# A one-core FNet-plus-MLP kernel: a second staging place, four turning places, an earlier split and an earlier build step

## The chip, the cores and the metric

The kernel runs on one core of a Trainium2 chip. The metric is the device time of one execution, in microseconds (us); a kernel's time is the median of several executions.

The engines are named as the profile names them: PE is TensorE (matmuls), PEld its weight loads, DVE VectorE, ACT ScalarE, POOL GpSimd, SP SyncE, which issues most DMAs. In the trace each engine runs its instructions in program order, and they wait for one another through semaphores. A DMA queue belongs to the engine that issues it; POOL's is `q0 software_dynamic`, SP's `q1 hardware_dynamic`.

## The reference

```python
x  = A_x                                   # 1 x 2048 x 640, fp32
xn = layernorm(x)                          # no scale, no shift
a, b = xn @ hid_re.T, xn @ hid_im.T        # 640 x 640 each
fnet = seq_re @ a - seq_im @ b             # 2048 x 2048 each
mlp  = gelu(xn @ w1 + b1) @ w2 + b2        # 640 -> 1536 -> 640
return x + fnet + mlp
```

All data are fp32 and one output of 2048 x 640 is returned.

## The kernel before

**Products.** Each fp32 operand is split into a high part, rounded to the matmul's fp32r format, and a low part, the rest. `split` (L154) does it with two instructions: ACT writes the high part (L160), DVE subtracts it from the source (L161). `product` (L274) then needs three matmuls, high x high (L277), high x low (L278) and low x high (L279), which add into one PSUM bank of 128 x 512. There are eight banks.

**Order of the work.** The schedule is written out by hand: an engine executes instructions in the order in which the Python code issues them, and there is no scheduler. The code interleaves the preparation of later stages with the matmuls of the present one. So a late instruction delays all that stands behind it on its engine, even where that has nothing to do with it.

1. *MLP, token blocks 0 and 1* (512 tokens each): hidden units by `hidden`, GELU, second matrix by `output`. The five outputs of a block lie in banks 3 to 7 (`oacc`).
2. *MLP, hidden layer of blocks 2 and 3*, six pairs of units q = 0 to 5, with a scheme that saves matmuls: `head(q)`, `mid(q)` and `finish(q)`. `PB[q]` says which banks a pair uses; the banks go from pair to pair, so a pair's first matmul into a bank waits until what lay there is read. In `mid`, DVE adds a shared term to two banks (L428, called from L850 and L851); the second of these reads bank z2, into which the first product of `finish` ("t4" with "a22", L855) then goes. `act` (L834) applies GELU and parks the results. Beside it `prep_w` (L396) turns and splits the hidden-dimension matrices and stores them through POOL's DMA queue (`wit`, L394), from five slots of one tile in rotation; it fills a slot again once its store has landed.
3. *MLP, second layer of blocks 2 and 3*: steps n = 0 to 23, 12 units each. Its moving operand is one of three places `HP`, filled by `split_h(p)` (L1053) for pair p of units. Block 2 gathers in banks 0 to 4, block 3 in banks 5, 6, 7, 3 and 4. At n = 12 block 3 starts with its first two units: first into banks 5, 6 and 7 (18 matmuls), then into banks 3 and 4 (12 matmuls), which have to be free of block 2's outputs by then.
4. *Sequence stage*: blocks of the sequence matrices, whose raw rows SP loads (`load_a`, L452) and DVE turns (`turn`, L484) into places `r01` and `rt2`, whose forms `form` (L511) splits.

**Beside stage 3: the builds.** `beside_second(n)` (L1130) issues, among the matmuls, eight builds of the normalised input's forms for stage 4. `load_xr(k)` (L543) loads two tiles of 128 x 640 from `xs` on SP's queue, the first four builds are `formed(k)` at n = 2, 4, 6 and 8: `build` (L561) computes an "ab" form of 128 x 2560 and a "c" form of 128 x 1792, and POOL's queue stores them to `forms_ab` and `forms_c` (L1122, L1123). The c form is put in the place that `homes_c` (L623) names; in the kernel before it is `xcst`, under the tag `tw1`, for each of the four, and the next build's first write there (ACT, L582) waits until the store of the one before has landed. What stands behind a build in program order, on ACT and on DVE: after the fourth (n = 8) come `split_h(6)` (n = 9, needed by PE at n = 12), parts a and b of build 4 (n = 9, from tiles loaded by `load_xr(4)`, issued at n = 6), `split_h(7)` (n = 11), and then the five outputs of block 2 (`outs(2, (3, 4, 0, 1, 2))`, n = 11).

**Outputs of a block.** `outs` (L861) calls `add_block` (L341) for each of five output banks: ACT adds the bias in place (L344), DVE turns the bank into a place `yt` (L347), POOL adds that to `xo` (L349). For block 1 the first output (bank 3) goes by itself (L1064), and the other four in `rest` (L1066) inside `mid(0)`, through the two halves of the tile `AB` in turn. `zs` is a tile of 128 x 3840, seven and a half places of 512 columns, with the sources of stage 2's operands.

**Turn to stage 4** (L1188 to L1273). When PE has done stage 3, ACT copies the five outputs of block 3 with their bias into `ob` (L1247); then follow build 7's part b (L1269: one subtraction and two splits), the turning of piece 2 into `rt2` (whose bytes hold weights that PE reads until the end of stage 3), and build 7's part c. ACT gets to what stands behind L1247 only when PE has finished block 3.

Of the kernel before, what the change touches and what calls it, by code (L numbers as in the profile page):

```python
# [11 lines left out]
F32R = mybir.dt.float32r  # L12
# [3 lines left out]
P = 128  # L16
# [10 lines left out]
def kernel(  # L27
# [43 lines left out]
    TB = 512  # L71
# [24 lines left out]
    NK = 4  # L96
# [57 lines left out]
    def split(hi, lo, src, perm=False):  # L154

        h, l, s = (hi, lo, src)
        if perm:
            h, l = chunked(hi), chunked(lo)
            s = src.rearrange("p (q c i) -> p q c i", q=Q, i=B)
        nc.scalar.activation(h, s, AF.Copy)  # L160
        nc.vector.tensor_tensor(l, s, h.bitcast(F32), op=ALU.subtract)  # L161
# [61 lines left out]
    AB = mr.tile([P, 2, TB], F32, name="ab")  # L223
# [117 lines left out]
    def add_block(dst, e, acc, name, eng=nc.gpsimd, bias=None, yt=None):  # L341

        if bias is not None:
            nc.scalar.activation(acc, acc, AF.Identity, bias=bias)  # L344
        if yt is None:
            yt = rows.tile([P, TB], F32, tag="yt", bufs=2, name=name)
        nc.vector.transpose(yt, acc)  # L347
        d = dst[:, :, e * B : (e + 1) * B]
        eng.tensor_tensor(d, d, yt.rearrange("p (n i) -> p n i", i=B), op=ALU.add)  # L349


    A = {}
# [74 lines left out]
    def add(dst, a, b, op=ALU.add):  # L427
        nc.vector.tensor_tensor(dst, a, b, op=op)  # L428
# [111 lines left out]
    builds = [(h, c) for h in (1, 0) for c in range(NK)]  # L540
# [20 lines left out]
    def build(k, what="abc"):  # L561
        h, c = builds[k]
        b0, b1_ = [r.rearrange("p (q c i) -> p c q i", q=Q, i=B) for r in xr[k]]
        if "a" in what:
            A["xab", c] = homes_ab[k]()
        if "c" in what:
            A["xc", c] = homes_c[k]()
        ab, xc = A["xab", c], A.get(("xc", c))
        if k == len(builds) - 1 and what == "b":
            A["sums"] = out_pool.tile([P, 2, 9 * P], F32, tag="zo", bufs=1, name="sums")  # L570
        tmp = A["sums"][:, (0, 1, 0, 1, 0, 0, 1, 1)[k]]

        def seen(ap):
            return ap.rearrange("p (c q i) -> p c q i", q=Q, i=B)

        n1, m2, t3, t4, b5 = (
            seen(tmp[:, lo * P : (lo + w) * P]) for lo, w in ((0, 2), (2, 2), (4, 2), (6, 2), (8, 1))
        )

        def part(dst, lo, w, src, negative=False):  # L580
            h_, l_ = (seen(dst[:, i, lo * P : (lo + w) * P]) for i in range(2))
            nc.scalar.activation(h_, src, AF.Copy, scale=-1.0 if negative else 1.0)  # L582
            if negative:
                nc.vector.scalar_tensor_tensor(
                    l_, src, -1.0, h_.bitcast(F32), op0=ALU.mult, op1=ALU.subtract
                )
            else:
                add(l_, src, h_.bitcast(F32), ALU.subtract)

        b11, b12, b21, b22 = b0[:, 0:4:2], b0[:, 1:5:2], b1_[:, 0:4:2], b1_[:, 1:5:2]  # L590
        if "b" in what:
            add(n1, b11, b12, ALU.subtract)
        if "a" in what:
            part(ab, 0, 3, b0[:, 0:5:2])
        if "c" in what:
            add(m2, b22, n1)
        if "a" in what:
            part(ab, 3, 3, b1_[:, 0:5:2])
        if "c" in what:
            add(t3, b22, b12, ALU.subtract)  # L600
        if "b" in what:
            part(ab, 8, 2, b22)
        if "c" in what:
            add(t4, m2, b21, ALU.subtract)
        if "b" in what:
            part(ab, 6, 2, n1)
        if "c" in what:
            add(b5, b1_[:, 4:5], b0[:, 4:5], ALU.subtract)
            part(xc, 0, 2, m2, True)
            part(xc, 2, 5, seen(tmp[:, 4 * P :]))  # L610


    def staged(lo):
        return lambda: A["asb"][:, lo : lo + 20 * P].rearrange("p (a b) -> p a b", a=2)

    def at_xab(c):
        return lambda: place(f"xab{c}", (P, 2, 10 * P))
# [2 lines left out]
        return lambda: A["kept", c]  # L620

    homes_ab = [staged(0), at_xab(0), at_xab(2), staged(0), at_xab(0), at_xab(1), at_xab(2), at_xab(3)]
    homes_c = [lambda: A["tw"].tile([P, 2, 7 * P], F32R, tag="tw1", bufs=1, name="xcst")] * NK  # L623
    homes_c += [lambda c=c: A["xcp", c // 2 * 2][:, c % 2] for c in range(NK)]

    zeros = rows.tile([P, TB], F32, tag="yt", bufs=2, name="zeros")
# [107 lines left out]
    def load_rq(q):  # L734
        if q >= NF // 2:
            return
        RQ[q] = A["xf"].tile([P, 4, 2 * P], F32, tag="rq", bufs=1, name=f"rq{q}")
        v = w1.rearrange("(q c i) f -> q i c f", q=Q, i=B)
        for k in range(Q):
            nc.sync.dma_start(RQ[q][k * B : (k + 1) * B], v[k, :, :4, 2 * q * P : 2 * (q + 1) * P])  # L740

    def sums_w1(q):
        if q >= NF // 2:
            return
        r = RQ[q]
        low = r[:, 0:2].rearrange("p c (g f) -> p g c f", g=2)
        high = r[:, :, P:].rearrange("p (k c) f -> p k c f", k=2)
        add(low, high, low, ALU.subtract)
        add(r[:, 2:4, P:], r[:, 2:4, P:], r[:, 0:2, :P], ALU.subtract)
        add(r[:, 2:4, :P], r[:, 2:4, :P], r[:, 2:4, P:], ALU.subtract)  # L750

    def split_w1(q):
        if q >= NF // 2:
            return
        TW[q] = A["tw"].tile([P, 2, 8 * P], F32R, tag=f"tw{q % 2}", bufs=1, name=f"tw{q}")
        split(TW[q][:, 0], TW[q][:, 1], RQ.pop(q).rearrange("p a b -> p (a b)"))
        TW[q] = TW[q].rearrange("p a (c f) -> p a c f", c=4)
# [22 lines left out]
    def pair(k, q, w, x_, first):  # L780
        n = 1 if x_ in ("oa", "ob") else 2
        for cc in range(n):
            f = FX[x_, cc]
            product(bank(k), weights(q, w, cc), (f[:, 0], f[:, 1]), first and cc == 0, cc == n - 1, not first)
# [49 lines left out]
    def act(q, blk, k):  # L834
        y, d, x2, z2, w_ = PB[q]
        src = ((x2, y), (z2, w_))[blk][k]
        u = 2 * q + k
        nc.scalar.activation(park(q, blk, k), bank(src), AF.Gelu_apprx_tanh, bias=b1c[:, u : u + 1])
# [14 lines left out]
    def finish(q):  # L853
        y, d, x2, z2, w_ = PB[q]
        pair(z2, q, "t4", "a22", False)  # L855
        pair(z2, q, "o1", "ob", False)
        pair(y, q, "b22", "s4", False)
        pair(y, q, "o2", "oa", False)
        pair(w_, q, "o2", "ob", False)

    def outs(t, order, yt=None, done=True):  # L861
        for n, e in enumerate(order):
            add_block(
                xo[t], e, oacc[t][e], f"ot{t}_{e}", bias=b2c[:, e : e + 1], yt=yt(n) if yt else None
            )
        for k, (c0, c1) in enumerate(YCOLS if done else ()):
            nc.sync.dma_start(ys[k][t], xo[t][:, :, c0:c1])
# [185 lines left out]
    def split_h(p):  # L1053

        blk, u = (0, 2 * p) if p < NF // 2 else (1, LATE[2 * (p - NF // 2)])
        h = HP[p % 3]
        split(h[:, :, 0], h[:, :, 1], both[blk, u])
        for k in range(2):
            HU[blk, u + k] = h[:, k]
# [4 lines left out]
    outs(1, (0,), yt=lambda n: AB[:, 0], done=False)  # L1064

    def rest():  # L1066
        outs(1, (2, 1, 3, 4), yt=lambda n: AB[:, (n + 1) % 2])

    mid(0, rest)
    forms_s4()  # L1070
    head(1)
# [4 lines left out]
    for q in range(1, NF // 2):  # L1076
        p = q - 1
        if not p % 2:
            act(p, 0, 0)
        sums_w1(q + 1)  # L1080
        act(p, 0, 1)

        def between():
            split_w1(q + 1)
            load_rq(q + 2)
            act(p, 1, 0)
            act(p, 1, 1)

        mid(q, between)
        if q < NF // 2 - 1:  # L1090
            head(q + 1)
        else:
            second(2, 0, 0, HU[0, 0])
            split_h(1)
            for u in (2, 3):
                split_w2(u)
                raw_w2(u + 4, u - 2)
        for k in late_steps.get(q, ()):
            prep_w(k)
        finish(q)  # L1100
        if q == 4:
            split_h(0)
            prep_w(14)
            for u in range(2, 6):
                raw_w2(u, u - 2)
# [96 lines left out]
    def fr_tile(shape, tag, name, dtype=F32):  # L1202
        return fr.tile(list(shape), dtype, tag=tag, bufs=1, name=name)
# [38 lines left out]
            nc.sync.dma_start(A[which, c][:, :, cols].bitcast(F32), src[c][:, :, cols])  # L1242


    ot = [fr_tile((P, 2, TB), tag, f"ob{k}") for k, tag in enumerate(("u1_0", "u2_0", "v1_0"))]
    for e in (3, 4, 0, 1, 2):
        nc.scalar.activation(ot[e // 2][:, e % 2], oacc[NT - 1][e], AF.Identity, bias=b2c[:, e : e + 1])  # L1247
# [18 lines left out]
    def late_block(e):  # L1266
        add_turned(xo[NT - 1][:, :, e * B : (e + 1) * B], turned(ot[e // 2][:, e % 2], f"ot{NT - 1}_{e}"))

    build(len(builds) - 1, "b")  # L1269
    A["rt2"] = place("rt2", (P, 2, 2, 2, TB), F32)  # L1270
    turn(2, 0)
    turn(2, 1)
# [370 lines left out]
    for kind, what in stages:  # L1643
        b = blocks.index(what) if kind == "s" else b
# [63 lines left out]
```

## Time and profile before

| | us |
|---|---|
| median of 3 executions | 864.68 (864.55 to 865.17) |
| the profiled execution's own time | 865.7 |
| its span, first to last instruction | 863.9 |
| PE busy | 845.8 |
| DVE busy | 659.7 |
| ACT busy | 354.3 |
| POOL busy | 45.1 |

The profile's times count from the start of the span. A timeline row gives start, duration, engine, line, operation, written tile <- read tiles, shapes, count of instructions that were merged into the row, and in brackets the idle time of the engine before it with what ended it. The end of a matmul is modelled, and matmuls overlap: in an unbroken run they start 0.23 us apart though each is shown 0.39 us long.

### The profile page before, as it was taken

The numbers are of one execution on the slowest core, as the hardware profiler recorded it, in microseconds if no ns is written. First come the engines' busy times: TensorE is split into PE (matmuls) and PEld (weight loads), VectorE is DVE, ScalarE is ACT, GpSimd is POOL, SyncE is SP. The second block draws the span as 40 slices with busy tenths as digits, with TensorE's granted clock in tenths as the row PEclk, the third lists the DMA queues.
The fourth block names the chain that finished last, engine by engine and source line by source line (L and its number), as shares of the span: only waits on it lengthen the run. The fifth ranks groups of instructions, "written<-read, shape, count | busy, mean of one in ns | idle before, by whom it ended". The sixth has DMA issues, their size and how long they took to land.

```text
span 863.9 us, 10322 instructions
## 1 busy us (share of the span) xinstructions
PE 845.8 (98%) x3711; PEld 696.9 (81%) x3711; DVE 659.7 (76%) x831; ACT 354.3 (41%) x495; POOL 45.1 (5%) x65
## 2 busy tenths in 40 slices
PE   8999999999999799999999999999999999999997
PEld 6888888878878588788888888888888888888885
DVE  7555756766658585988988787998977898885686
ACT  7353634455665444344434333332322423223241
POOL 0000312021211030000000000000000000000000
PEclk9999999999999899999999999999999999999999
DMA  6757798747669976939663659854665869804464
GB/s 183 218 146 185 167 228 233 189 90 191 199 225 371 329 155 138 191 97 231 150 168 86 175 145 307 212 108 125 170 184 175 256 176 233 310 19 177 122 180 95
DMA packets 209219, 158.45 MB, mean 183 GB/s; under 512 B 82896, under 2 KB 182736, under 8 KB 208656
## 3 DMA queue, kind: packets, MB, share of 16 engines
q1 hardware_dynamic: 199936, 136.16, 61.5%
q0 software_dynamic: 3952, 20.71, 6.0%
q10 hardware_dynamic: 5280, 0.92, 0.5%
q8 instruction: 29, 0.48, 0.2%
q14 instruction: 22, 0.18, 0.1%
HBM read 114.76 MB, written 42.99 MB: 183 GB/s over the span
## 4 chain that ended last, share of the span: by engine, by line
PE 87%; issue 6%; DVE 2%; DMA 2%; POOL 1%; ACT 1%; SPq 0%; POOLq 0%; ACTq 0%; DVEq 0%
PE banks L278 26%; PE banks L279 26%; PE banks L277 26%; PE banks L301 9%; DMA forms_c<-xcst 1%; POOL wit L394 1%; DMA x<-in_A_x_dram 0%; DVE rt L488 0%; DMA raw<-in_A_dft_seq_re_dram 0%; POOL xo L349 0%; PE banks L664 0%; DVE hs L161 0%; DVE st L185 0%; DVE wz L428 0%; POOL forms_ab L1122 0%
## 5 line engine op out<-in xcount | busy, mean ns | idle before, releaser
L278 PE MATMUL banks<-as,xab 128*128 128x512 f32 x411 | 160.0, 389 | 0.8 <-DVE as L161 0.8
L277 PE MATMUL banks<-as,xab 128*128 128x512 f32 x411 | 159.9, 389 | 0.0
L279 PE MATMUL banks<-as,xab 128*128 128x512 f32 x411 | 159.9, 389 | 0.0
L160 ACT ACTIVATE as<-r 128x1024 fp32r<-128x1024 f32 x80 | 85.1, 1064 | 175.9 <-PE banks L279 148.3
L161 DVE TENSOR_TENSOR as<-r,as 128x1024 fp32r<-128x1024 f32 x80 | 97.2, 1216 | 38.7 <-ACT as L160 38.7
L278 PEld LDWEIGHTS banks<-as,xab 128*128 128x128 f32 x411 | 77.1, 188 | 17.2 <-DVE as L161 1.3
L277 PEld LDWEIGHTS banks<-as,xab 128*128 128x128 f32 x411 | 77.1, 188 | 16.2
L279 PEld LDWEIGHTS banks<-as,xab 128*128 128x128 f32 x411 | 77.1, 188 | 16.0
L277 PE MATMUL banks<-as,xc 128*128 128x512 f32 x224 | 87.1, 389 | 0.0
L278 PE MATMUL banks<-as,xc 128*128 128x512 f32 x224 | 87.1, 389 | 0.0
L279 PE MATMUL banks<-as,xc 128*128 128x512 f32 x224 | 87.1, 389 | 0.0
L160 ACT ACTIVATE as<-rt 128x1024 fp32r<-128x1024 f32 x32 | 34.1, 1064 | 69.8 <-PE banks L279 57.8
L301 PE MATMUL banks<-xtt,xab 128*128 128x512 f32 x240 | 56.7, 390 | 0.0
L301 PEld LDWEIGHTS banks<-xtt,xab 128*128 128x128 f32 x240 | 44.9, 188 | 9.5 <-DVE xtt L161 0.2
L277 PEld LDWEIGHTS banks<-as,xc 128*128 128x128 f32 x224 | 42.0, 188 | 8.8
L278 PEld LDWEIGHTS banks<-as,xc 128*128 128x128 f32 x224 | 42.0, 188 | 8.7
L279 PEld LDWEIGHTS banks<-as,xc 128*128 128x128 f32 x224 | 42.0, 188 | 8.7
L161 DVE TENSOR_TENSOR as<-rt,as 128x1024 fp32r<-128x1024 f32 x32 | 38.8, 1213 | 5.3 <-ACT as L160 5.3
L488 DVE STREAM_TRANSPOSE r<-raw 128x1024 f32<-128x1024 f32 x32 | 39.5, 1240 | 3.4 <-PE banks L279 2.8
L160 ACT ACTIVATE as<-u 128x1024 fp32r<-128x1024 f32 (+1 forms) x24 | 22.1, 921 | 48.1 <-PE banks L279 48.1
L320 DVE TENSOR_TENSOR hs<-ab,hs 128x512 fp32r<-128x512 f32 x24 | 17.6, 732 | 31.6 <-ACT hs L318 29.4
L161 DVE TENSOR_TENSOR as<-u,as 128x1024 fp32r<-128x1024 f32 (+1 forms) x24 | 24.9, 1043 | 18.8 <-ACT as L160 18.8
(333 smaller groups left out, 1631.6 us busy)
## 6 DMA issues: line engine op xcount, KB each, us to landing
raw<-in_A_dft_seq_re_dram SPq DMA_DIRECT2D x64, 256.0 KB, 5.2
raw<-in_A_dft_seq_im_dram SPq DMA_DIRECT2D x64, 256.0 KB, 5.1
ws<-wit SPq DMA_DIRECT2D x15, 384.0 KB, 4.7
x<-in_A_x_dram SPq DMA_DIRECT2D x16, 320.0 KB, 4.1
xs<-x SPq DMA_DIRECT2D x64, 80.0 KB, 1.8
xo<-in_A_x_dram SPq DMA_DIRECT2D x16, 320.0 KB, 6.1
xab<-wit SPq DMA_DIRECT2D x13, 384.0 KB, 4.4
wit<-wstp POOLq DMA_DIRECT2D x12, 384.0 KB, 4.2
```

The costliest lines, as they stand in the source:

```text
L160: nc.scalar.activation(h, s, AF.Copy)
L161: nc.vector.tensor_tensor(l, s, h.bitcast(F32), op=ALU.subtract)
L277: nc.tensor.matmul(acc, wh, mh, start=first, stop=False, skip_group_check=goes_on)
L278: nc.tensor.matmul(acc, wh, ml, start=False, stop=False, skip_group_check=goes_on)
L279: nc.tensor.matmul(acc, wl, mh, start=False, stop=last, skip_group_check=goes_on)
L301: nc.tensor.matmul(acc, W1[i][:, a, j * P : (j + 1) * P], XT[j][:, b], start=n == 0, stop=n == len(steps) - 1)
L320: nc.vector.tensor_tensor(hs[:, 1], a, hs[:, 0].bitcast(F32), op=ALU.subtract)
L394: nc.gpsimd.dma_start(wits[w][j], t[:, :, :n].bitcast(F32))
L488: nc.vector.transpose(held(pieces[g][2], u).rearrange("p c (n i) -> p c n i", i=B), r.rearrange("p n (c i) -> p c n i", i=B))
```

## The change

There are four edits. None changes what is computed, and the number of matmuls, splits, stores and loads stays the same.

1. The c form of the fourth build goes to the place with tag `tw0`; the first three stay in `tw1`. `tw0` held stage 2's weights of even pairs, and after them the parked units 8 to 11 of block 2, which `split_h(4)` and `split_h(5)` read (n = 5 and n = 7).
2. The four outputs of block 1 in `rest` are turned into places 4, 5, 0 and 1 of `zs` in place of the two halves of `AB`.
3. `split_h(0)` is issued after `finish(3)`, ahead of pair 4's work, in place of after `finish(4)`, where it stood in front of `prep_w(14)`.
4. Build 7's part b is issued ahead of the five ACT copies into `ob`, in place of behind them.

```diff
-    homes_c = [lambda: A["tw"].tile([P, 2, 7 * P], F32R, tag="tw1", bufs=1, name="xcst")] * NK
+    homes_c = [
+        lambda c=c: A["tw"].tile([P, 2, 7 * P], F32R, tag="tw0" if c == 3 else "tw1", bufs=1, name=f"xcst{c}")
+        for c in range(NK)
+    ]
...
     def rest():
-        outs(1, (2, 1, 3, 4), yt=lambda n: AB[:, (n + 1) % 2])
+        free = (4, 5, 0, 1)
+        outs(1, (2, 1, 3, 4), yt=lambda n: A["zs"][:, free[n] * TB : (free[n] + 1) * TB])
...
         finish(q)
+        if q == 3:
+            split_h(0)
         if q == 4:
-            split_h(0)
             prep_w(14)
...
+    build(len(builds) - 1, "b")
     ot = [fr_tile((P, 2, TB), tag, f"ob{k}") for k, tag in enumerate(("u1_0", "u2_0", "v1_0"))]
     for e in (3, 4, 0, 1, 2):
         nc.scalar.activation(ot[e // 2][:, e % 2], oacc[NT - 1][e], AF.Identity, bias=b2c[:, e : e + 1])
...
-    build(len(builds) - 1, "b")
     A["rt2"] = place("rt2", (P, 2, 2, 2, TB), F32)
     turn(2, 0)
     turn(2, 1)
     build(len(builds) - 1, "c")
```

In the built kernels PE's, POOL's and SP's instructions stand in the same order before and after; on ACT and DVE the only instructions that change place are those of edits 3 and 4.

## The prediction

> **What bounds the kernel now.** I read the page first, then PE's waits, then the timelines of each engine around each wait.
>
> ```profile
> span 863.9 us, 10322 instructions
> PE 845.8 (98%) x3711; PEld 696.9 (81%) x3711; DVE 659.7 (76%) x831; ACT 354.3 (41%) x495; POOL 45.1 (5%) x65
> ...
> PE banks L277 <- ACT hs L160: 5.7, 1, 5.7
> ...
> PE banks L278 <- DVE as L161: 0.8, 1, 0.8
> PE banks L277 <- DVE banks L428: 0.8, 1, 0.8
> PE banks L277 <- ACT banks L794: 0.6, 1, 0.6
> ```
>
> PE is busy all but 18.1 us, and the change leaves its matmuls as they are. So an edit is worth the waits of PE that it takes away, less those that it makes. Beyond the start-up there are few: one of 5.7 us, and some below 1 us. A second, third and fourth view place them.
>
> ```profile
> 292.38 0.39 PE L279 MATMUL banks<-xtt,rt 128*128 128x512 f32 x1
> 298.49 0.80 PE L277 MATMUL banks<-hs,xc01w 128*128 128x512 f32 x1 [5.72 <-ACT hs L160]
> 299.75 0.79 PE L278 MATMUL banks<-hs,xc01w 128*128 128x512 f32 x1 [0.46 <-DVE hs L161]
> 300.34 0.63 PE L279 MATMUL banks<-hs,xc01w 128*128 128x512 f32 x1
> ...
> 305.40 0.39 PE L277 MATMUL banks<-hs,xc01w 128*128 128x512 f32 x1
> ...
> 284.38 11.96 DMA forms_c<-xcst
> ...
> 288.30 0.29 DVE L428 TENSOR_TENSOR asb<-xr,xr 128x128 f32<-128x128 f32 x1
> 298.47 1.23 DVE L161 TENSOR_TENSOR hs<-pb,hs 128x1024 fp32r<-128x1024 f32 x1
> ...
> 296.44 1.04 ACT L582 ACTIVATE xcst<-asb 128x256 fp32r<-128x256 f32 x2 [10.22 <-DMA forms_c<-xcst]
> 297.39 1.04 ACT L160 ACTIVATE hs<-pb 128x1024 fp32r<-128x1024 f32 x1
> ...
> 360.00:860.00 500.00, 497.68 (x2195) 411.53 (x2194) 420.00 (x386) 172.50 (x175) 0.00 (x0) 1.00 0.64 171
> ```
>
> The last row is a window's busy times (and instructions) of PE, PEld, DVE, ACT and POOL, then PE's granted clock. It gives the unbroken pace: 2195 matmuls in 500 us, 0.228 us each. PE ends block 2 with the matmul at 292.38 and could start block 3 at 292.61, but starts at 298.49, and its 19th matmul there, the first into bank 3, comes at 305.40 where the pace would give 292.61 + 18 x 0.228 = 296.7. **This pause costs 8.7 us**: 5.9 before the first matmul and 2.8 after it, for the wait on DVE and for matmuls that start 0.43 us apart (300.34 to 303.32 holds seven such steps). Its cause stands in the other rows. ACT, in the fourth build, waits 10.22 us until the third build's c form has left the one staging place, a store of 11.96 us. `split_h(6)` stands behind it on ACT and DVE, and PE needs that.
>
> **The change part by part.**
>
> *Edit 1, second staging place.* In the order of the built instructions, ACT's and DVE's waits on that store are gone and none is added; the readers of `tw0` stand earlier on the same engines. DVE has the fourth build's sums ready at 288.6 (row 288.30). ACT then needs 1.04 at most for the c form's two parts (row 296.44) and 1.04 for `hs`: 290.7. DVE follows, 1.23 for its half: 291.9. PE's first two matmuls need them at 292.6 and 292.8, so this wait ends, with 0.9 us to spare. What is late next stands behind it on both engines: build 4's first parts, `split_h(7)`, and block 2's outputs, whose banks 3 and 4 PE needs with its 19th matmul.
>
> ```profile
> L558 SPq DMA_DIRECT2D xr<-xs x2: 345/360/376, 282.2 to 282.6; - x2
> ...
> DMA to landing us min/median/max: 8.5/10.0/11.6
> ...
> 298.34 1.23 ACT L582 ACTIVATE xab<-xr 128x384 fp32r<-128x384 f32 x3
> 300.39 1.05 ACT L160 ACTIVATE xtt<-pb 128x1024 fp32r<-128x1024 f32 x1
> ...
> 301.55 1.22 DVE L161 TENSOR_TENSOR xtt<-pb,xtt 128x1024 fp32r<-128x1024 f32 x1
> 302.69 1.31 DVE L347 STREAM_TRANSPOSE ot<-banks 128x512 f32<-128x512 f32 x2
> ```
>
> Build 4's two tiles are issued at 282.2 and 282.6 and take 8.5 and 11.6 us: the second lands at **294.2**. In the kernel before that was no matter, ACT began these parts at 298.34. Now it is there at about 291 and waits for the second tile. From 294.2: two of the three parts in row 298.34, 0.85; a fourth, smaller part, some 0.3 by their size; `split_h(7)` on ACT, 1.05, then on DVE, 1.22, with ACT's first bias beside it; then the first turning of row 302.69, 0.7. That makes 298.3 for bank 3. Bank 4 follows 0.6 later, and PE wants it three matmuls, 0.7, later. So PE runs on from 292.6, and pauses 1.6 us ahead of its 19th matmul, at 298.3 in place of 305.40: **7.1 us earlier, not 8.7**. By the kernel's own rows this end does not move with PE, only with the landing.
>
> Does that pause slow the matmuls after it? Row 300.34 shows half pace after 5.72 us of idling; waits of under 1 us (rows below) cost one longer matmul, 0.50 for 0.39. Bounds: 0.1 and 2.8 us, or 856.3 and 859.0 at the end. I take 0.1, since 1.6 is nearer to 0.8 than to 5.7. The Trainium skill, "TensorE: Matmul & The Clock Gate", Part 1 on the clock gate, has a threshold for this: the clock halves after an idle window of about 3.4 us. By it the sum stays at 0.1; the rows above agree on both sides of it, and none shows a pause between 0.8 and 5.7.
>
> *Edit 2, four turning places.*
>
> ```profile
> 182.21 1.36 DVE L347 STREAM_TRANSPOSE ab<-banks 128x512 f32<-128x512 f32 x2 [1.28 <-ACT banks L344]
> ...
> 185.58 0.72 DVE L347 STREAM_TRANSPOSE ab<-banks 128x512 f32<-128x512 f32 x1 [0.52 <-POOL xo L349]
> 186.22 1.26 DVE L428 TENSOR_TENSOR banks<-banks,fifth 128x512 f32<-128x512 f32 x2
> 176.13 1.29 DVE L161 TENSOR_TENSOR xtt<-zs,xtt 128x512 fp32r<-128x512 f32 x2 [0.43 <-ACT xtt L160]
> ...
> 187.39 1.79 DVE L161 TENSOR_TENSOR xtt<-zs,xtt 128x512 fp32r<-128x512 f32 x2
> ...
> 185.11 0.50 PE L277 MATMUL banks<-r,tw 128*128 128x512 f32 x1 [0.39 <-DVE ab L347]
> 187.54 0.50 PE L277 MATMUL banks<-r,tw 128*128 128x512 f32 x1 [0.77 <-DVE banks L428]
> ...
> 200.59 0.85 DVE L372 STREAM_TRANSPOSE wz<-wz 128x640 f32<-128x640 f32 x1 [1.75 <-DMA wz<-in_A_dft_hid_im_dram]
> ...
> 209.79 1.29 DVE L428 TENSOR_TENSOR banks<-banks,fifth 128x512 f32<-128x512 f32 x2
> ...
> 212.16 0.39 PE L277 MATMUL banks<-r,tw 128*128 128x512 f32 x1
> ```
>
> A wait costs its idle time, 0.16 of overlap (0.39 less 0.23) and 0.11 in the longer first matmul: 0.66 and 1.04 here, 1.7 together. Without the wait for POOL, DVE turns the four banks 0.64 apart from 182.21 (two in 1.36, starts 0.64 apart) and begins the additions at 184.8 in place of 186.22, ending them at 186.05. PE reaches the second of these points at 185.9, so 0.3 stays and 1.4 goes. Twenty-five us later there is a new bound: the same additions of pair 2 end at 211.08, in a run of DVE work behind a load (`wz`, row 200.59) that waits for POOL's last addition and the store of `xo`, which edit 2 doesn't bring forward. PE would need them at 212.16 - 1.4 = 210.8: 0.5 comes back, **0.9 stays**. DVE's next two subtractions took 1.79 beside POOL's additions, where two of the same shape took 1.29 before these; if in their new place they hold POOL up by as much, half a us, the load and all behind it come later and 0.4 stays. The Trainium skill, "SBUF — State Buffer", section "Who interferes with whom", says that a VectorE instruction with two SBUF inputs and a GpSimd one that reads SBUF exclude each other for their whole length; row 187.39 agrees, and by it 0.4 would be the value. I keep both ends, 0.4 and 0.9.
>
> *Edit 3, earlier `split_h(0)`.*
>
> ```profile
> 230.04 1.60 DVE L428 TENSOR_TENSOR rq<-rq 128x512 f32<-128x512 f32 x3
> 233.92 1.29 DVE L428 TENSOR_TENSOR banks<-banks,fifth 128x512 f32<-128x512 f32 x2
> 242.31 1.22 DVE L161 TENSOR_TENSOR hs<-pa,hs 128x1024 fp32r<-128x1024 f32 x1
> ...
> 236.64 0.39 PE L277 MATMUL banks<-r,tw 128*128 128x512 f32 x1
> ```
>
> DVE's subtraction, 1.22, goes from 242.31 to just ahead of row 230.04, and must first wait some 0.5 for ACT's half (1.04, the shape of row 297.39, behind ACT's part of `prep_w`). It delays, one behind the other, the sums `rq`, their split and the two additions: their end goes from 235.21 to 237.0. PE needs it at 236.64, a new wait of 0.3 and with its 0.27 **about 0.5 lost**. PE's wait of 0.6 on L794 stays, since `prep_w` behind these is delayed as much. What it gives: three of POOL's stores leave a little sooner, and with them the chain of loads that ends in stage 3. Bounds: 0.6 lost, 0 if ACT's half comes sooner.
>
> Edits 2 and 3 thus nearly cancel for PE. At 298.3 they count only as they bring the landing at 294.2 forward: between 0 and 0.6; I take 0.3.
>
> *Edit 4, build 7's part b.*
>
> ```profile
> 342.40 3.01 ACT L1247 ACTIVATE ob<-banks,b2c 128x512 f32<-128x512 f32 x5 [4.38 <-PE banks L279]
> ...
> 346.43 2.37 DVE L488 STREAM_TRANSPOSE rt<-raw 128x1024 f32<-128x1024 f32 x2
> ...
> 355.58 0.50 PE L278 MATMUL banks<-as,xab 128*128 128x512 f32 x1 [0.83 <-DVE as L161]
> ```
>
> ACT idles 4.38 us ahead of row 342.40, which covers part b's two ACT splits. DVE then turns piece 2 when PE frees `rt2`, at about 342.4, and not at 346.43: 4 us sooner, and what follows up to PE's wait goes some 3 us sooner (part c still waits for ACT's copies). PE's wait at 355.58 goes: 0.83 + 0.16 + 0.11 = **1.1**. The loads that `turn` issues go out sooner too, on a queue that serves nothing else there. If ACT idled there no longer, the edit would cost what part b takes on ACT, under 1 us.
>
> **Sum.** Edit 1 to the 19th matmul 7.1, less 0.1, plus 0.3, plus edit 4's 1.1: 8.4. The profiled execution took 865.7, 1.8 beyond its span, and gives 857.3; it lies 1.0 above the median of 864.68, which gives **856.3**.
>
> **The rivals.**
>
> *Nothing takes the pause's place* (12%): the loads land sooner, or `outs` isn't behind them. Then 8.7 + 1.1 and up to 0.9 of edit 2: 854.0 to 854.9. Against it stands the 11.6 row, and that the order on ACT and DVE is fixed.
>
> *The new pause is dearer* (20%): the landing comes 1 to 2 us later, as the fourth c form's store now starts some 8 us sooner and shares the DMA engines, or the matmuls after it run at half pace. 857.3 to 859.
>
> *The second place frees nothing* (3%): its store or its earlier readers end as late as the first's. Then only edits 2 to 4 count, 0 to 1.5: 863.2 to 864.7. The missing wait in the built order speaks against it.
>
> *Slower* (2%): with PE's longest rest gone, its clock is granted less for the rest of the run. Some 566 us follow; a clock of 0.985 would take back 566 x (1/0.985 - 1) = 8.6, all that is gained, and below it the kernel is slower than before: 867.9 at 0.98. Window 360 to 860 speaks against: clock 1.00 with no rest in it.
>
> **How the numbers follow.** The forecast's own range is 855.3 to 857.3 (63%): the landing's 0.6, edit 2's and edit 3's bounds. Range for 8 in 10: 854.0 to 858.3, with most of the first two rivals. A measurement tells 0.2%, 1.7 us, from no change: faster 0.95, same 0.03, slower 0.02.
>
> **What would show it.** PE's wait on ACT `hs` gone from its waits, and ACT's on the store of `xcst` in build 4; a wait of 1 to 2 us of PE on DVE `ot` L347 at 18 matmuls into block 3, ended by ACT's wait on `xr`; no wait on DVE `as` near 345; waits of about 0.2 to 0.5 on L428 near 186, 211 and 236. It would be wrong if PE waited for `hs` still, if ACT never waited on `xr`, or if a wait of over 1 us appeared beyond 300.

## The result, and the profile after

| | before | after |
|---|---|---|
| median of 5 executions beside one another, us | 865.17 (864.55 to 866.05) | 858.26 (856.76 to 861.04) |
| ratio, with its 95% interval | | 0.992 (0.990 to 0.994) |
| the profiled execution's own time, us | 865.7 | 858.26 |
| its span, us | 863.9 | 856.5 |

The kernel is 6.9 us faster. The forecast was 856.3, so 8.4 below; the measured time is at the upper end of its range (854.0 to 858.3). The changed kernel was run again twice, with 7 executions each beside the kernel before: medians 860.66 and 859.73, where the kernel before had 866.22 and 866.07. Over all 19 executions the median is 859.27, and they lie between 856.76 and 866.40. This scatter of nearly 10 us is new; in those three places the kernel before lay between 864.3 and 868.3. Most of what follows is about it.

First the page of the kernel after, then PE's waits in it:

```profile
span 856.5 us, 10320 instructions
PE 843.5 (98%) x3711; PEld 695.7 (81%) x3711; DVE 661.5 (77%) x831; ACT 353.7 (41%) x495; POOL 45.5 (5%) x65
```

```profile
PE banks L667 <- DVE xp L208: 2.4, 1, 2.4
PE banks L648 <- DVE warm L639: 1.9, 1, 1.9
PE banks L277 <- DVE ot L347: 1.5, 1, 1.5
PE banks L277 <- ACT banks L797: 1.0, 1, 1.0
```

The wait of 5.7 us on ACT `hs` is gone, and so are those on DVE `as`, on L428 and on `ab` (0.4). In their place stands one of 1.5 on DVE `ot` L347, where the prediction put it. L667 and L648 belong to the start-up. L797 is L794 of the kernel before, since the change adds three lines.

The timeline of the kernel after, around the start of block 3:

```profile
289.80 1.05 ACT L160 ACTIVATE hs<-pb 128x1024 fp32r<-128x1024 f32 x1
290.88 1.23 DVE L161 TENSOR_TENSOR hs<-pb,hs 128x1024 fp32r<-128x1024 f32 x1
292.04 0.53 ACT L582 ACTIVATE xab<-xr 128x384 fp32r<-128x384 f32 x1 [1.19 <-DMA xr<-xs]
295.10 0.83 ACT L582 ACTIVATE xab<-xr 128x384 fp32r<-128x384 f32 x2 [2.54 <-DMA xr<-xs]
297.10 2.94 ACT L344 ACTIVATE banks<-banks,b2c 128x512 f32<-128x512 f32 x5
298.37 1.30 DVE L347 STREAM_TRANSPOSE ot<-banks 128x512 f32<-128x512 f32 x2
299.13 0.50 PE L277 MATMUL banks<-hs,xc01w 128*128 128x512 f32 x1 [1.46 <-DVE ot L347]
```

`hs` is ready at 292.11, before PE needs it. Then ACT waits twice for a tile of `xr`, and 4.0 us after the second tile's start there (295.10) PE gets bank 3. The load itself, in the view of its line:

```profile
L558 SPq DMA_DIRECT2D xr<-xs x2: 345/360/375, 282.6 to 283.1; - x2
...
DMA to landing us min/median/max: 9.3/10.7/12.0
```

The second tile is issued at 283.06 and lands at 295.08.

**Where the time came from.** I set the start of each matmul in one trace against the same matmul in the other. The first transposes wait longer for the load of `x` (2.4 us in place of 1.2), so PE begins 1.24 later; no edit touches this. After block 1's outputs it stands at -0.17 (edit 2: 1.41 gained), in pair 5, at the wait on L797, at +0.80 (edit 3: about 1.0 lost), at the 19th matmul of block 3 at -6.27 (edit 1: 7.07 gained), past the matmul that stood at 355.58 at -7.27 (edit 4: 1.0 gained), at the end at -7.4. Without the start-up that is 8.66, against 8.4 forecast.

### The profile page after: what moved, and what is told of

Read it like the earlier page. It is cut to its first block, busy times and chain, and to the rows that moved or that the text cites. A ratio compares the mean times of both kernels' runs of the same rounds, so it can differ in the third digit from the quotient of the medians.

```text
span 856.5 us, 10320 instructions
## 1 busy us (share of the span) xinstructions
PE 843.5 (98%) x3711; PEld 695.7 (81%) x3711; DVE 661.5 (77%) x831; ACT 353.7 (41%) x495; POOL 45.5 (5%) x65
## 4 chain that ended last, share of the span: by engine, by line
PE 84%; issue 7%; DMA 4%; POOL 2%; DVE 2%; ACT 1%; SPq 1%; POOLq 0%; DVEq 0%; ACTq 0%
PE banks L277 25%; PE banks L278 25%; PE banks L279 25%; PE banks L301 10%; DMA xr<-xs 1%; POOL wit L394 1%; DMA wz<-in_A_dft_hid_im_dram 1%; DMA x<-in_A_x_dram 1%; DMA forms_c<-xcst 1%; POOL xo L349 1%; DMA ys<-xo 0%; SPq L364 0%; PE banks L667 0%; DMA rq<-in_B_w_dram 0%; DVE xtt L161 0%
## 5 line engine op out<-in xcount | busy, mean ns | idle before, releaser
L488 DVE STREAM_TRANSPOSE rt<-raw 128x1024 f32<-128x1024 f32 x32 | 38.8, 1230 | 0.9 <-PE banks L279 0.8
```

What stands on the lines that cost most here:

```text
L488: nc.vector.transpose(held(pieces[g][2], u).rearrange("p c (n i) -> p c n i", i=B), r.rearrange("p n (c i) -> p c n i", i=B))
```

## The experiments

**Theory A**, the prediction's: PE's new pause is set by the landing of build 4's second tile `xr`, and edits 2 and 3 count only as far as they move that landing. **Theory B**: each wait of PE that goes or comes counts in full. **Rival C**: block 2's outputs make the pause by themselves. All kernels are the changed kernel with the edit shown, if nothing else is said.

### Edit 1 alone (e1_place_alone)

The kernel before with this one hunk:

```diff
-    homes_c = [lambda: A["tw"].tile([P, 2, 7 * P], F32R, tag="tw1", bufs=1, name="xcst")] * NK
+    homes_c = [
+        lambda c=c: A["tw"].tile([P, 2, 7 * P], F32R, tag="tw0" if c == 3 else "tw1", bufs=1, name=f"xcst{c}")
+        for c in range(NK)
+    ]
```

> Edit 1 alone, the second staging place. Theory A (the pause ahead of bank 3 in block 3 is set by the landing of build 4's second tile xr, and what stands ahead of it counts only as it moves that landing): the first matmul of block 3 follows the last of block 2 without a pause, PE waits about 2 to 2.5 us on DVE ot L347 at the 19th matmul of block 3, since PE is 0.6 us earlier there than in the whole change's trace only if edits 2 and 3 brought it so much; the end is 7.0 to 7.1 us below the kernel before, a ratio of about 0.992, so the whole change less edit 4's 1.0. The waits of the kernel before on POOL xo near 186, on L428, and on DVE as near 355 stay. Theory B (each PE wait adds up in the end time): 8.7 less the new pause of about 1.8, so 6.9; the two are the same here in time. Rival C (the landing is not it, the pause is made by block 2's own outputs): a PE wait on ot with ACT's waits on xr absent or under 0.3 us.

Measured: 861.63 (12 executions, 858.5 to 868.0) beside 866.2, ratio 0.995 (0.993 to 0.997). So 4.6 and not 7. The profiled execution took 867.96, longer than the median of the kernel before, and its timeline tells why:

```profile
301.06 0.83 ACT L582 ACTIVATE xab<-xr 128x384 fp32r<-128x384 f32 x2 [2.13 <-DMA xr<-xs]
...
305.08 0.79 PE L277 MATMUL banks<-hs,xc01w 128*128 128x512 f32 x1 [7.56 <-DVE ot L347]
```

The load was issued at 283.2, as in the kernel after, but landed 17.8 us later and not 12.0. The pause is 7.6, and bank 3 comes at 305.08, hardly sooner than in the kernel before (305.40). Half pace then costs more. Three windows of this trace (us, busy time and instructions of PE, PEld, DVE, ACT, POOL, PE's granted clock, DMA share, GB/s):

```profile
298.00:300.00 2.00, 0.00 (x0) 0.00 (x0) 0.98 (x2) 0.52 (x1) 0.00 (x0) 0.95 0.98 406
300.00:310.00 10.00, 4.92 (x12) 3.86 (x13) 6.17 (x10) 6.09 (x12) 4.84 (x4) 0.50 0.14 58
310.00:311.00 1.00, 1.00 (x6) 0.82 (x5) 1.00 (x2) 0.54 (x2) 1.00 (x2) 0.98 0.00 0
```

The granted clock is 0.50 from 299.8, still within the pause, to 310.0. From the 19th matmul on, 49 steps from one matmul to the next took 13.56 us where they take 11.25 in the kernel after: 2.3 more. Block 3's first matmul comes without a pause, as expected; the size of the gain was not foreseen by either theory. C is out: the pause has moved with the load.

### Edits 2, 3 and 4 without edit 1 (e2_without_place)

```diff
-        lambda c=c: A["tw"].tile([P, 2, 7 * P], F32R, tag="tw0" if c == 3 else "tw1", bufs=1, name=f"xcst{c}")
-        for c in range(NK)
-    ]
+    homes_c = [lambda: A["tw"].tile([P, 2, 7 * P], F32R, tag="tw1", bufs=1, name="xcst")] * NK
```

> Edits 2, 3 and 4 without edit 1. The old pause stays: PE waits 5 to 6 us on ACT hs L160 ahead of block 3, ended by the store of the third build's c form. Theory A: that store's landing is a landing too, so edits 2 and 3 count only as they bring it forward, 0 to 0.6 us, and edit 4 gives 1.0: 1.0 to 1.6 us below the kernel before. Theory B (each PE wait counts by itself): edit 2 gives 1.4, edit 3 takes 1.0, edit 4 gives 1.0: 1.4 below. What tells them apart is the length of the pause on hs: by A it grows by as much as PE came earlier (about 0.4), by B it stays at 5.7.

Measured: 864.37 beside 866.2, ratio 0.9979 (0.9971 to 0.9988), 1.8 less. PE's waits of this run:

```profile
PE banks L277 <- ACT hs L160: 5.5, 1, 5.5
```

By theory A the old pause should have grown by what PE gained ahead of it. It is 5.5 where it was 5.7. This speaks for B, weakly, since the times of the two overlap.

### The change without edit 3 (e3_without_split)

```diff
-        if q == 3:
-            split_h(0)
         if q == 4:
+            split_h(0)
             prep_w(14)
```

> The whole change without edit 3 (split_h(0) back behind finish(4)). The PE waits on L428 near 236 go and the one on ACT L797 near 246 is again 0.6: PE comes to stage 3 about 1.0 us earlier than in the whole change. Theory A: the landing of xr decides, so the pause at the 19th matmul of block 3 is longer by about what PE gained, and the end is 0 to 0.4 us below the whole change's. Theory B: the end is 1.0 us below the whole change's, with the pause unchanged at 1.5 to 1.9.

Measured: 859.77 (6 executions, 856.1 to 864.3) beside 866.2, ratio 0.9925 (0.990 to 0.995). The scatter hides the 1.0 in question, so the times decide nothing; the trace says more. Rows of its timeline, then two of its windows:

```profile
295.14 0.83 ACT L582 ACTIVATE xab<-xr 128x384 fp32r<-128x384 f32 x2 [2.66 <-DMA xr<-xs]
...
299.17 0.50 PE L277 MATMUL banks<-hs,xc01w 128*128 128x512 f32 x1 [2.94 <-DVE ot L347]
```

```profile
299.00:300.00 1.00, 0.83 (x3) 0.72 (x4) 0.71 (x2) 1.00 (x3) 0.75 (x1) 0.91 0.95 396
300.00:304.00 4.00, 4.00 (x12) 3.16 (x12) 2.39 (x4) 1.36 (x4) 4.00 (x4) 0.60 0.04 16
```

PE reached stage 3 1.4 us earlier than in the kernel after (0.5 of that from the start-up), and the load was issued 1.5 earlier, at 281.55. But this time it took 13.6 us. After a wait of 2.94 the clock was 0.91 in the microsecond in which PE resumed and 0.60 in the next four. Single microseconds between show 0.50, so that is half pace for 0.2 + 3.2 = 3.4 us from 299.8 on; 11 matmuls started in those four microseconds where 17 do in the kernel after (the counts of the views take in those that were already running). It cost 1.6 more.

### The loads in the other order (e4_xr_first)

```diff
-        if n == 6:
-            load_xo(2)
         if n in (2, 4, 6, 8):
             formed(n // 2 - 1)
             load_xr((2, 3, 4, 6)[n // 2 - 1])
+        if n == 6:
+            load_xo(2)
```

> The whole change with one thing moved: at n = 6 the loads of build 4's tiles are issued ahead of the load of block 2's xo, and not behind it. Theory A: both tiles land 1 to 2 us sooner, ACT's wait on xr in build 4 shrinks by as much, and so does PE's wait on DVE ot L347 at the 19th matmul of block 3, from 1.5 to 0.5 or nothing: 1 to 1.8 us below the whole change's time, unless xo's later landing holds POOL's additions in block 2's outputs up, which PE doesn't wait for. Rival C (block 2's own outputs make the pause): no change in the pause, and a time within 0.3 of the whole change's. A third possibility: the queue serves the loads side by side, so that the order of issue moves the landing by under 0.3 us, and nothing is decided; then the same build issued behind the outputs is to decide.

Measured: 863.91 beside 866.2, ratio 0.997 (0.996 to 0.998); 4.6 *above* the whole change's median of 859.27. The load's view (first fence), PE's waits and the timeline:

```profile
DMA to landing us min/median/max: 3.4/5.4/7.3
```

```profile
PE banks L277 <- ACT xtt L160: 4.3, 1, 4.3
...
PE banks L278 <- DVE xtt L161: 1.6, 1, 1.6
```

```profile
303.33 6.39 POOL L349 TENSOR_TENSOR xo<-xo,ot 128x512 f32<-128x512 f32 x5 [13.09 <-DMA xr<-xs]
...
304.65 0.72 DVE L347 STREAM_TRANSPOSE ot<-banks 128x512 f32<-128x512 f32 x1 [9.59 <-POOL xo L349]
...
310.04 0.80 PE L277 MATMUL banks<-xtt,xc 128*128 128x512 f32 x1 [4.34 <-ACT xtt L160]
```

Half of the expectation came true: the tile lands 7.3 us after its issue in place of 12.0, and PE's pause ahead of bank 3 is gone. But now `xo` is the load behind. Its last piece lands at 302.84 and POOL's first addition starts at 303.33 (the profile names the load `xr`, which landed at 303.37, after that addition had begun; `xo` fits). There are two places `ot`, so DVE stands for 9.59 us in front of the third output, and the split that PE needs at 310 stands behind it. "PE doesn't wait for POOL's additions" was wrong: it does, through DVE.

### The whole change twice more (e5_whole_again, e10_whole_beside)

No edit.

> The whole change once more, as the measure for the three beside it and as a second trace of the same kernel. Theory A (the pause at the 19th matmul of block 3 is set by the landing of build 4's second tile, which varies from execution to execution): the median lies within 1.5 us of 858.3, the executions scatter by 3 to 5 us where those of the kernel before scatter by 1.5 to 3, and the pause in this trace differs from 1.5 as the landing does from 12.0 us after its issue, one for one. Rival C (block 2's own outputs make the pause): the pause is again 1.5, whatever the landing.

> The whole change beside it on the same chip, as the measure for its time and its scatter. By theory A the median lies between 857.5 and 861, the executions scatter by 4 us or more, and the pause ahead of bank 3 in this trace is the time from xr's landing less what PE still had to do, 1.5 to 8 us.

Measured: 860.66 (857.17 to 866.40) beside 866.22, ratio 0.994 (0.992 to 0.997); and 859.73 (856.98 to 864.91) beside 866.07, ratio 0.994 (0.991 to 0.996). The timelines of the first, and of the second:

```profile
293.62 0.83 ACT L582 ACTIVATE xab<-xr 128x384 fp32r<-128x384 f32 x2 [2.52 <-DMA xr<-xs]
...
297.65 0.50 PE L277 MATMUL banks<-hs,xc01w 128*128 128x512 f32 x1 [1.85 <-DVE ot L347]
```

```profile
299.45 0.83 ACT L582 ACTIVATE xab<-xr 128x384 fp32r<-128x384 f32 x2 [2.56 <-DMA xr<-xs]
...
303.47 0.79 PE L277 MATMUL banks<-hs,xc01w 128*128 128x512 f32 x1 [6.15 <-DVE ot L347]
```

With these, five traces have this pause; the table adds the last experiment's as a sixth row. Issue and landing are from the view of the load's line, the rest from rows like those above:

| trace | `xr` issued | landed | after | PE's bank 3 | from landing | PE's wait |
|---|---|---|---|---|---|---|
| whole (the result) | 283.06 | 295.08 | 12.0 | 299.13 | 4.05 | 1.46 |
| edit 1 alone | 283.20 | 301.04 | 17.8 | 305.08 | 4.04 | 7.56 |
| without edit 3 | 281.55 | 295.12 | 13.6 | 299.17 | 4.05 | 2.94 |
| whole again | 281.35 | 293.60 | 12.3 | 297.65 | 4.05 | 1.85 |
| whole beside | 282.68 | 299.43 | 16.7 | 303.47 | 4.04 | 6.15 |
| whole rows | 281.67 | 293.35 | 11.7 | 297.40 | 4.05 | 1.17 |

From the landing to PE it is 4.04 to 4.05 us in every trace, while the landing itself moves by 7.7. That settles which load sets the pause.

**Why the landing scatters.** In the trace each of these loads counts its semaphore up in 16 parts. (The Trainium skill, "DMA: Bandwidth & Descriptors", section "Why a DMA increments its semaphore by 16 and not by 1": one part for each DMA engine, which finish independently.) The times of some:

```text
                                  1st part  15th    16th
xo, fourth piece   whole          287.61    288.85  289.08
                   edit 1 alone   287.32    288.79  294.61
                   whole beside   287.30    288.44  292.69
xr, second tile    whole          292.94    294.54  295.08
                   edit 1 alone   292.84    295.83  301.04
                   whole beside   292.55    294.55  299.43
```

In the long executions 15 parts of `xr` are there 11.9 and 12.6 us after the issue, where the first has them after 11.5; the last is 5 us behind the rest, and so it was already in the load ahead of `xr` in the queue, by 4 to 6 us. Two rows of the DMA view of the kernel after, 288 to 296 us (packets, MB, share of 16 engines):

```profile
q0 software_dynamic: 311, 2.48, 74.2%
q1 hardware_dynamic: 346, 0.79, 27.2%
```

Once POOL's stores (q0) run, SP's loads (q1) get as many packets but a third of the bytes. The Trainium skill, "DMA: Bandwidth & Descriptors", section "Queues, rings and completion order", says that each DMA engine goes round its queues packet by packet; these counts agree. By that rule a part of `xo` that still waits on one engine when the stores begin is served in small packets between large ones. That this is what held the one part up is argued, not shown.

### Build 4 behind the outputs (e6_build_behind)

```diff
-        if n == 9:
-            build(4, "ab")
         if n == 11:
             outs(2, (3, 4, 0, 1, 2))
+            build(4, "ab")
```

> The whole change with build 4's parts a and b issued behind block 2's outputs (both at n = 11) and not ahead of split_h(7) (n = 9). Theory A: nothing ahead of bank 3 waits for xr any more; the PE wait on DVE ot L347 is gone, block 3 runs at 0.23 us a matmul from its first, and the time is 1.7 to 2.5 us below the whole change's, about 856.3, with the executions within 2 us of one another. ACT's waits on xr move behind the outputs, where 6 us are left before PE needs what stands behind them. Rival C: the pause stays 1.5 and the time is within 0.3 of the whole change's. Third possibility, as with the loads in the other order: a later wait of PE on xtt L160 near 310 takes its place and the time is the same or above.

Measured: 855.90 (4 executions, 855.24 to 856.69) beside 866.22, ratio 0.988 (0.986 to 0.990). PE's waits, all of them:

```profile
PE banks L648 <- DVE warm L639: 1.9, 1, 1.9
PE banks L277 <- ACT banks L797: 1.3, 1, 1.3
PE banks L667 <- DVE xp L208: 0.8, 1, 0.8
```

The pause is gone, and with it the scatter: 1.5 us between the executions in place of 9. The load still lands 12.0 us after its issue, at 294.53; ACT now begins these parts at 295.22, and waits for nothing. This is 3.4 below the whole change's median of 859.27, more than the 1.7 to 2.5 expected, which were reckoned from a pause of 1.5; in most executions of the whole change it must have been longer, by their times.

### The same without edit 3, and without edits 2 and 3 (e7, e8)

The first has the diffs of e6_build_behind and e3_without_split, the second also this:

```diff
-        free = (4, 5, 0, 1)
-        outs(1, (2, 1, 3, 4), yt=lambda n: A["zs"][:, free[n] * TB : (free[n] + 1) * TB])
+        outs(1, (2, 1, 3, 4), yt=lambda n: AB[:, (n + 1) % 2])
```

> The same without edit 3 (split_h(0) back behind finish(4)). With no landing between, PE's waits add up: those near 236 (0.4) and 246 (1.3 in place of 0.75) cost edit 3 about 1.0, so this kernel ends 1.0 us below the one with build 4 behind the outputs, about 855.3. If edit 3's earlier stores matter beyond block 3's start (a landing that still sets the end), the two differ by under 0.3.

> The same without edits 2 and 3: block 1's outputs again turned in two places. The waits of PE on ab L347 (0.4) and on L428 (0.8) near 185 are back: 1.4 us above the run without edit 3 alone, so within 0.5 of the one with edits 2 and 3 both. If edit 2 counted only through the landing, the difference would be under 0.5.

Measured: 854.90 (854.25 to 856.20), ratio 0.987 (0.985 to 0.989), and 856.72 (856.23 to 857.76), ratio 0.989 (0.987 to 0.991). By these medians **edit 3 costs 1.0** (855.90 against 854.90) and **edit 2 brings 1.8** (856.72 against 854.90). They are medians of four executions each, and those of the first pair overlap, so the sizes are rough; the run without both was to lie within 0.5 of the run with both and lies 0.8 above. The traces, set against one another matmul by matmul from the end of the start-up to the last matmul, give 1.4 for edit 3 (0.8 of it in the wait on L797, which varies from trace to trace), and for edit 2 1.4 near 186, of which 1.0 is left at the end. So neither is lost on the way to the end. The page of the first and its wait on L797, and two waits of the second:

```profile
span 852.5 us, 10320 instructions
PE 842.1 (99%) x3711; PEld 695.3 (82%) x3711; DVE 661.2 (78%) x831; ACT 354.1 (42%) x495; POOL 45.6 (5%) x65
```

```profile
PE banks L277 <- ACT banks L797: 0.4, 1, 0.4
```

```profile
PE banks L277 <- DVE banks L428: 0.8, 1, 0.8
PE banks L277 <- DVE ab L347: 0.4, 1, 0.4
```

With edits 1, 2 and 4 and build 4 behind the outputs, the kernel at 854.90 is the best one of this study: 4.4 below the whole change's median.

### `xo` in whole rows (e9_whole_rows)

Block 2's `x` is loaded as rows of 10 KB in place of 640-byte pieces; the tile then holds other values, so block 2 of the output gets the wrong `x` added.

```diff
+    def load_xo_whole(t):
+        xo[t] = out_pool.tile([P, NB, DQ], F32, tag="zo", bufs=1, name=f"xo{t}")
+        for q in range(Q):
+            rows = x[t * TB + q * P : t * TB + (q + 1) * P].rearrange("(p n) d -> p (n d)", p=B)
+            nc.sync.dma_start(xo[t][q * B : (q + 1) * B].rearrange("p n d -> p (n d)"), rows)
...
         if n == 6:
-            load_xo(2)
+            load_xo_whole(2)
```

> The whole change, with block 2's x loaded at n = 6 as whole rows: the same four loads of 320 KB to the same tile, but each partition gets one piece of 10 KB in place of 16 pieces of 640 bytes. This changes what the tile holds, so block 2 of the output gets the wrong x added; the work of every engine stays. Theory A, with the landing late because the load of x ahead of xr on SP's queue is made of small pieces: the four pieces land sooner, xr lands 2 to 5 us sooner after its issue (7 to 10 in place of 12.0), the PE wait on DVE ot L347 shrinks to under 0.5 or goes, and the time is 1.5 to 2 us below the first whole run, about 856.3, with executions within 2 us of one another. If the piece size does not matter, only the bytes, the landing stays near 12, the pause at 1.5 or more and the scatter at 4 or more. If the queue of the stores takes the time that the smaller load leaves, the landing moves by under 1 us and the pause by as much.

Measured: 856.98 (856.64 to 858.42) beside 866.07, ratio 0.990 (0.989 to 0.992), where the whole change on the same chip took 859.73. The landing came only 0.3 sooner after its issue (11.7), and the pause of 1.17 stayed, as the third case of the expectation had it. But the five executions lie within 1.8 us. So the small pieces don't make the usual landing late. That they make it scatter follows from the times of these five executions beside seven of the whole change; with whole rows there is one trace, so no trace shows that a late part no longer comes.

## Why the prediction was right or wrong, point by point

*Edit 1.* The mechanism was right in each of its steps: `hs` in time, ACT's two waits on `xr`, `split_h(7)` and the outputs behind it, the pause at the 19th matmul. From the landing to bank 3 I had worked out 4.1 us (294.2 to 298.3); it is 4.05. In the profiled execution the edit gave 7.07 up to the 19th matmul, forecast 7.1; the pause is 1.46, forecast 1.6, since PE and the landing both came 0.8 to 0.9 later. **What failed is one term: the landing at 294.2.** I took a duration of one execution of the kernel before, 11.6 us, as fixed. There it decided nothing. In the kernel after it decides, and in six traces it is 11.7 to 17.8. The rival "the new pause is dearer" had 20%, with a landing 1 to 2 us later or half pace behind it. By their times 14 of the 19 executions were at it or beyond: 3 of the result's five took over 857.8, and 11 of the other 14 over 858.8, which is its 857.3 raised by the 0.5 and by the 1.4 to 1.5 by which the kernel before beside them lay above 864.68. It should have been the forecast, in a range up to 866. That the measured time came out inside the range is luck in part. As a gain the range was 6.4 to 10.7; the result's is 6.9, those of the two later places are 5.6 and 6.3. And the profiled execution had a short landing, 12.0, without which its sum would not have fitted so well.

*Half pace.* At 0.1 the cost of a short pause was right where the pause was short: after 1.46 and 1.85 us one longer matmul, 0.50. But 2.94 already cost half pace (clock 0.60 in the row above), 1.6 us, and 6.15 and 7.56 cost 2.0 and 2.3. So the point from which it does lies, in these traces, between 1.85 and 2.94, where I had only 0.8 and 5.7. The Trainium skill, "TensorE: Matmul & The Clock Gate", Part 1, has about 3.4 us of idling; the trace with 2.94 disagrees, since that shorter wait was enough. The same part says that the clock is decided in windows of about 3.4 us that run on by themselves; the half pace of 3.4 us that set in after PE had resumed agrees.

*"Edits 2 and 3 count only through the landing (0 to 0.6; took 0.3)."* Wrong, since the load is issued earlier by as much as PE comes earlier, and its landing moves along, apart from its scatter. From the matmul at `head` of pair 5 that waits for L794 to the issue of the load it is 37.07 us before (245.56 to 282.63), 36.70 after (246.36 to 283.06), and 36.6 to 37.0 in the other five traces of the table, where that matmul lies between 244.46 and 246.19. Both edits therefore count: 1.4 gained and 1.0 lost in the result's trace. That they nearly cancel, at 0.4 where the sum had 0.3, hid the error.

*Edit 2.* 1.4 gained near 186, as forecast. The wait expected near 211, which was to take back 0.5, did not come in the kernel after: DVE's additions end at 211.8 and PE runs without a break (0.1 to 0.3 in some of the other runs). That DVE's next two subtractions beside POOL's additions would be slower was right, by more than I gave:

```profile
183.45 2.51 DVE L347 STREAM_TRANSPOSE zs<-banks 128x512 f32<-128x512 f32 x4 [1.28 <-ACT banks L344]
185.89 1.27 DVE L428 TENSOR_TENSOR banks<-banks,fifth 128x512 f32<-128x512 f32 x2
187.06 3.23 DVE L161 TENSOR_TENSOR xtt<-zs,xtt 128x512 fp32r<-128x512 f32 x2
...
210.54 1.29 DVE L428 TENSOR_TENSOR banks<-banks,fifth 128x512 f32<-128x512 f32 x2
```

3.23 us where 1.79 stood. POOL's last addition beside them took 1.73 where the others take 1.29, so it was held up by 0.4; PE waited for neither.

*Edit 3.* Forecast at 0.5, it costs 1.0. The new waits near 236 were there, 0.4 together, and DVE's wait for ACT's half, forecast at some 0.5, is 0.50. What was mis-sized is the wait near 245, said to stay at 0.6:

```profile
230.50 1.23 DVE L161 TENSOR_TENSOR hs<-pa,hs 128x1024 fp32r<-128x1024 f32 x1 [0.50 <-ACT hs L160]
...
235.51 1.29 DVE L428 TENSOR_TENSOR banks<-banks,fifth 128x512 f32<-128x512 f32 x2
...
244.24 0.42 ACT L160 ACTIVATE wstp<-wz 128x256 fp32r<-128x256 f32 x1 [0.21 <-DMA wit<-wstp]
...
246.36 0.50 PE L277 MATMUL banks<-xtt,tw 128*128 128x512 f32 x1 [1.04 <-ACT banks L797]
```

It is 1.04. ACT stands ahead of it in `prep_w`, a little of the time for a store of `wit` to land. In the seven traces with edit 3 the wait on this line is 0.4 to 1.5, in the five without it 0.3 to 0.6. What makes it vary was not tried.

*Edit 4.* As forecast: ACT idles ahead of its copies, piece 2 is turned at once when PE has finished (336.20), the wait on `as` is gone, 1.0 for 1.1.

```profile
336.20 2.37 DVE L488 STREAM_TRANSPOSE rt<-raw 128x1024 f32<-128x1024 f32 x2 [0.78 <-PE banks L279]
336.28 3.00 ACT L1253 ACTIVATE ob<-banks,b2c 128x512 f32<-128x512 f32 x5 [1.32 <-PE banks L279]
```

*The other rivals.* "Nothing takes the pause's place" did not happen, but the run with build 4 behind the outputs shows its time: 855.90, at a distance of 10.3 from the kernel before beside it, where 9.8 to 10.7 was worked out. "The second place frees nothing" and "slower by a lower clock" are out: the wait on `hs` is gone, and the clock of the whole execution is 0.998 after.

## What to carry to other kernels

When a wait is taken away and a load is next behind it, ask how much that load's time varies, not only what it was once: the time of a landing that nobody waited for, read from one trace, is one value out of a spread. The cure was cheap here: put the outputs that PE waits for ahead of the build that waits for the load, and both the pause and the scatter are gone. And a gain ahead of a pause isn't lost in it when the load that ends the pause is issued by engines that keep pace with PE.

## What the runs showed of the hardware that was not expected

- The time of a 320 KB load behind 1.28 MB of small pieces on the same queue is set by the slowest of its 16 parts: 15 parts within 12.6 us in the three traces with their parts shown, the last at 12.0, 16.7 and 17.8 us. Issued ahead of the small pieces the same load took 7.3.
- 640-byte pieces in place of 10 KB ones cost the load itself little (its four loads land within 9.3 us of the first issue with whole rows, 9.7 with small pieces in the result's trace), but the executions scattered by 7.9 us (7 of them) beside 1.8 (5 with whole rows).
- A wait of PE of 2.94 us was enough for half pace, which set in 0.6 us after PE had resumed; one of 1.85 was not. The half pace lasted 3.4 us there, and 10.2 us around the end of the wait of 7.56.
